# Linear attention and a snake MLP on one core: attention of each batch interleaved with the MLP products of earlier tokens

## The chip, the cores and the metric

The kernel runs on one core of one Trainium2 chip. The metric is the device time of one execution in microseconds, median over several runs. TensorE multiplies matrices; its results go to a memory of their own, PSUM, and a copy out of PSUM is called an eviction below. VectorE and ScalarE do arithmetic by rows and read PSUM and SBUF, the memory of the operands; GpSimd is given operands in SBUF alone in these kernels; DMA queues move data from and to the chip's main memory. The engines run side by side, each in its own order of instructions, and wait for one another by semaphores.

## The reference, cut to what matters

```python
# attention: batch 8, heads 8, sequence 576, head_dim 64
q_s = exp(q) / sum(exp(q), axis=-1)          # over head_dim (the maxima cancel)
k_s = exp(k) / sum(exp(k), axis=2)           # over the sequence
kv  = einsum('bhsd,bhse->bhde', k_s, v)
x   = einsum('bhsd,bhde->bhse', q_s, kv)     # then 4608 tokens x 512
# MLP: d_model 512, d_ff 2048
h = x @ w_in
g = h + sin(alpha * h)**2 / alpha            # "the gate" below
out = g @ w_out
```

## The kernel before: the parts that the change and the argument touch

Both kernels make bf16 operands, let exp go without its maximum, and keep x transposed (`xT`, model dimension on the partitions) for the MLP. Before, attention of all batches comes first, by chunks of 128 tokens and four heads; a scheduler orders the instructions.

```python
for b in range(B):
    for h0 in range(0, H, HG):                      # HG = 4 heads
        for ci, (s0, sc) in enumerate(s_sizes):     # 128, 128, 128, 128, 64 tokens
            # k on the sync queue, q (and v below) on the scalar queue: runs of 256 bytes
            nc.sync.dma_start(out=kqc[:sc, :HG], in_=k[b, h0:h0 + HG, s0:s0 + sc, :].rearrange("hh s d -> s hh d"))
            nc.scalar.activation(kqcb[:sc], kqc[:sc], AX.Exp)
            nc.vector.tensor_reduce(qs[:sc], qc[:sc], axis=AXL.X, op=ALU.add)
            nc.vector.reciprocal(qs[:sc], qs[:sc])
            nc.vector.tensor_tensor(qcb[:sc], qc[:sc], ...)                # divide q
            ...  # two transposes, each with its VectorE copy; sums of k by a product with ones
            ...  # VectorE cast of v; four kv products, 64 columns each
        ...      # VectorE: kv / sum of k, per head
        for si, sblk in enumerate(range(0, S, 512)):                       # per head
            nc.tensor.matmul(o_ps[pb:pb + D, :nfree], kv_sb[pb:pb + D, kp],
                             q_sbT[pb:pb + D, kp, sblk:sblk + nfree], start=True, stop=True)
            nc.vector.tensor_copy(xT_sb[pb:pb + D, ko, mbase:mbase + nfree], o_ps[pb:pb + D, :nfree])
...              # weights: one load and one ScalarE cast each
for mo in range(nMouter):                           # nine tiles of 512 tokens
    for ni in range(nN):                            # 16 blocks of 128 hidden units
        for ki in range(nK):                        # 4 products: h
            nc.tensor.matmul(h_ps, win_sb[:, ki, ...], xT_sb[:, ki, m0:m0 + MF], ...)
        nc.scalar.activation(s_sb, h_ps, AX.Sin, scale=a_col)
        nc.scalar.activation(s_sb, s_sb, AX.Square)
        nc.vector.scalar_tensor_tensor(g_all[:, ni], in0=s_sb, scalar=inva_col, in1=h_ps, ...)
    for j in range(MF // 128):                      # 4 x 16 output products
        ...
```

## Time and profile before

Time before: 480.73 us (median of 4 runs, 480.59 to 480.87).

| Stage of the kernel before | us | busiest engine |
|---|---|---|
| attention, eight batches | 0 to 217 | VectorE, 175.5 us busy |
| MLP, nine tiles | 217 to 479 | TensorE, 98% busy |

The view by windows gives the busy time of each engine in a stretch of the span, with the number of instructions, then the recorded clock of TensorE (1.00 is full speed), the DMA engines' share and GB/s. These are three stretches of the kernel before:

```profile
0.00:217.00 217.00, 100.73 (x768) 53.75 (x769) 175.50 (x706) 65.28 (x84) 0.70 (x6) 1.00 0.72 170
217.00:222.00 5.00, 4.97 (x13) 1.78 (x13) 0.00 (x0) 3.02 (x5) 0.00 (x0) 1.00 0.00 0
222.00:479.00 257.00, 252.12 (x1141) 108.94 (x1139) 126.88 (x180) 158.91 (x286) 0.00 (x0) 1.00 0.10 37
```

The order of the columns is TensorE products, weight loads, VectorE, ScalarE, GpSimd. The first stretch is attention: VectorE is the busiest at 175.5 of 217 us. The third is the MLP at TensorE's pace. The second is the first 5 us of the MLP.

The chain of waits of the kernel before, in order of time (start, length, what), two pieces of the MLP:

```profile
264.67 11.74 PE outp L169 x54
293.15 11.74 PE outp L169 x54
```

They repeat every 28.48 us: that is one tile, 128 products at 217 ns (11.74 us for 54) and little else.

### The profile page before, as it was taken

To read this page: it belongs to the slowest core of one execution; us is meant where nothing else is said; L and a number is where in the kernel's file an instruction comes from. 1 tells how busy PE (TensorE), PEld (TensorE's weight loads), DVE (VectorE), ACT (ScalarE), POOL (GpSimd) and SP (SyncE) were. 2 spreads that over 40 slices of the span, in tenths; PEclk is the share of its full clock that TensorE was granted. 3 is DMA by queue.
4 is the path that set the end of the run, shared out by engine and by line. 5 is a ranking of instruction groups with operands and counts; after the bars stand their busy time and mean duration, and the time that the engine had idled before them with its cause. 6 is when DMAs were issued, how large, how long until landed. Compare 5 with 4: busy or idle time off the path is not lost.

```text
span 479.4 us, 5928 instructions
## 1 busy us (share of the span) xinstructions
PE 357.8 (75%) x1920; PEld 164.5 (34%) x1920; DVE 302.4 (63%) x886; ACT 227.2 (47%) x373; POOL 0.7 (0%) x6
## 2 busy tenths in 40 slices
PE   1152355555555555559999999999999999999996
PEld 0120222222222222323444444444444444444442
DVE  2395589999999999994626355362644536455462
ACT  2130132322222227537829286491937739195680
POOL 0000000000000000000000000000000000000000
PEclk9999999999999999999999999999999999999999
DMA  9899697766677674500020100102011020101102
GB/s 266 259 205 339 169 174 178 171 155 152 149 157 175 149 164 93 123 2 0 0 89 0 67 22 26 64 0 87 2 45 46 3 86 0 67 22 46 44 1 88
DMA packets 124303, 46.54 MB, mean 97 GB/s; under 512 B 117104, under 2 KB 117104, under 8 KB 123760
## 3 DMA queue, kind: packets, MB, share of 16 engines
q1 hardware_dynamic: 47984, 27.28, 19.3%
q10 hardware_dynamic: 76288, 18.88, 18.2%
q8 instruction: 15, 0.25, 0.2%
q14 instruction: 16, 0.13, 0.1%
HBM read 36.71 MB, written 9.44 MB: 96 GB/s over the span
## 4 chain that ended last, share of the span: by engine, by line
PE 36%; DVE 25%; ACT 22%; DMA 9%; issue 7%; ACTq 0%; SPq 0%
PE outp L169 22%; ACT s_sb L162 13%; DVE xT_sb L124 10%; ACT s_sb L163 8%; DMA kqc<-in_q_dram 8%; DVE q_sbT L92 5%; PE h_ps L157 4%; PE o_ps L119 4%; PE qcT_ps L90 3%; DVE qcb L85 3%; PE kvps L102 3%; DVE v_sb L98 2%; DVE kv_sb L113 1%; DVE g_all L164 1%; DVE qs L82 1%
## 5 line engine op out<-in xcount | busy, mean ns | idle before, releaser
L164 DVE SCALAR_TENSOR_TENSOR g_all<-s_sb,inva_sb,h_ps 128x512 bf16<-128x512 f32 x144 | 102.0, 745 | 71.0 <-ACT s_sb L163 71.0
L157 PE MATMUL h_ps<-xT_sb,win_sb 128*128 128x512 bf16 x576 | 136.7, 383 | 2.5 <-DVE xT_sb L124 0.9
L169 PE MATMUL outp<-wout_sb,g_all 128*128 128x512 bf16 x576 | 135.3, 379 | 0.1
L162 ACT ACTIVATE s_sb<-h_ps,alpha_sb 128x512 f32<-128x512 f32 x144 | 94.0, 714 | 84.7 <-PE h_ps L157 84.7
L78 ACT ACTIVATE kqcb<-kqc 128x512 bf16<-128x512 f32 (+1 forms) x80 | 50.0, 629 | 137.5 <-DMA vf<-in_v_dram 39.7
L163 ACT ACTIVATE s_sb<-s_sb 128x512 f32<-128x512 f32 x144 | 85.7, 659 | 0.5
L157 PEld LDWEIGHTS <-win_sb 128*128 128x128 bf16 x576 | 56.6, 98 | 77.7 <-issue 17.5
L169 PEld LDWEIGHTS <-g_all 128*128 128x128 bf16 x576 | 54.2, 98 | 71.1 <-DVE g_all L164 9.4
L173 DVE COPY o_sb<-outp 128x512 f32<-128x512 f32 x36 | 24.9, 691 | 61.6 <-PE outp L169 61.6
L119 PE MATMUL o_ps<-q_sbT,kv_sb 64*64 64x64 bf16 (+1 forms) x128 | 37.1, 437 | 30.0 <-DVE kv_sb L113 24.7
L124 DVE CAST xT_sb<-o_ps 64x512 bf16<-64x512 f32 (+1 forms) x128 | 52.7, 451 | 8.2 <-PE o_ps L119 6.0
L102 PE MATMUL kvps<-v_sb,kqcb 128*64 128x64 bf16 (+1 forms) x320 | 25.9, 242 | 32.6 <-DVE v_sb L98 32.6
L90 PE MATMUL qcT_ps<-identb,qcb 128*128 128x128 bf16 (+1 forms) x160 | 29.7, 288 | 22.9 <-DVE qcb L85 21.6
L82 DVE TENSOR_REDUCE qs<-kqcb 128x4 f32<-128x256 bf16 (+1 forms) x80 | 32.3, 405 | 8.9 <-ACT kqcb L78 8.9
L102 PEld LDWEIGHTS <-kqcb 128*64 128x64 bf16 (+1 forms) x320 | 21.7, 135 | 44.4 <-issue 44.1
L93 PE MATMUL ksps<-ones,kqcb 128*128 128x1 bf16 (+1 forms) x160 | 14.2, 173 | 29.9 <-ACT kqcb L78 29.8
L92 DVE COPY q_sbT<-qcT_ps 128x128 bf16<-128x128 bf16 (+1 forms) x160 | 27.1, 210 | 14.5 <-PE qcT_ps L90 11.0
L85 DVE TENSOR_TENSOR qcb<-kqcb,qs 128x256 bf16<-128x256 bf16 (+1 forms) x80 | 33.3, 417 | 0.5
L119 PEld LDWEIGHTS <-kv_sb 64*64 64x64 bf16 x128 | 12.3, 134 | 41.1 <-DVE kv_sb L113 29.1
L98 DVE CAST v_sb<-vf 128x256 bf16<-128x256 f32 (+1 forms) x80 | 20.9, 265 | 6.8 <-DMA vf<-in_v_dram 6.7
L93 PEld LDWEIGHTS <-kqcb 128*128 128x128 bf16 (+1 forms) x160 | 9.5, 110 | 43.5 <-ACT kqcb L78 34.6
L90 PEld LDWEIGHTS <-qcb 128*128 128x128 bf16 (+1 forms) x160 | 10.4, 109 | 33.0 <-DVE qcb L85 32.0
(16 smaller groups left out, 52.8 us busy)
## 6 DMA issues: line engine op xcount, KB each, us to landing
out_dram<-o_sb SPq DMA_DIRECT2D x36, 256.0 KB, 2.0
kqc<-in_k_dram SPq DMA_DIRECT2D x64, 128.0 KB, 2.9
kqc<-in_q_dram ACTq DMA_DIRECT2D x64, 128.0 KB, 3.1
vf<-in_v_dram ACTq DMA_DIRECT2D x64, 128.0 KB, 2.8
tmp<-in_moe_w_in_dram SPq DMA_DIRECT2D x1, 4096.0 KB, 13.6
tmp<-in_moe_w_out_dram SPq DMA_DIRECT2D x1, 4096.0 KB, 18.4
kqc<-in_k_dram SPq DMA_DIRECT2D x16, 64.0 KB, 3.0
kqc<-in_q_dram ACTq DMA_DIRECT2D x16, 64.0 KB, 3.2
```

Source lines behind the costliest of these rows:

```text
L78: nc.scalar.activation(kqcb[:sc], kqc[:sc], AX.Exp)
L85: nc.vector.tensor_tensor(qcb[:sc], qc[:sc], qs[:sc].unsqueeze(2).to_broadcast([sc, HG, D]), op=ALU.mult)
L90: nc.tensor.transpose(qcT_ps[:, :sc], qcb[:sc, kp * 2:(kp + 1) * 2], identb[:sc, :sc])
L92: nc.vector.tensor_copy(q_sbT[:, kp, s0:s0 + sc], qcT_ps[:, :sc])
L102: nc.tensor.matmul(kv_ps_l[kp][pb:pb + D, hi % 2], kcb[:sc, hi], v_sb[:sc, hi], start=(ci == 0), stop=(ci == NC - 1))
L119: nc.tensor.matmul(o_ps[pb:pb + D, :nfree], kv_sb[pb:pb + D, kp], q_sbT[pb:pb + D, kp, sblk:sblk + nfree], start=True, stop=True)
L124: nc.vector.tensor_copy(xT_sb[pb:pb + D, ko, mbase:mbase + nfree], o_ps[pb:pb + D, :nfree])
L157: nc.tensor.matmul(h_ps, win_sb[:, ki, ni * 128:(ni + 1) * 128], xT_sb[:, ki, m0:m0 + MF], start=(ki == 0), stop=(ki == nK - 1))
L162: nc.scalar.activation(s_sb, h_ps, AX.Sin, scale=a_col)
L163: nc.scalar.activation(s_sb, s_sb, AX.Square)
L164: nc.vector.scalar_tensor_tensor(g_all[:, ni], in0=s_sb, scalar=inva_col, in1=h_ps, op0=ALU.mult, op1=ALU.add)
L169: nc.tensor.matmul(outp, g_all[:, ni, j * 128:(j + 1) * 128], wout_sb[:, ni, :], start=(ni == 0), stop=(ni == nN - 1))
```

## The change

The intent is to fill TensorE, which was half idle in attention, by running attention of batch t+1 among the MLP products of tile t, and to make attention cheaper: one load for a whole batch of q, k or v, nine neighbouring tokens on one partition (runs of 2304 bytes), few wide operations, kv products of even and odd heads on the upper and lower 64 rows of the array. The order of instructions is now written by hand: what the source issues first comes first on each engine. The heart of the change (the helpers are ordinary):

```diff
-            for ci, (s0, sc) in enumerate(s_sizes):
-                ...                                       # the loops shown above
+    ctx.enter_context(tc.manual_schedule())
+    stage = ... bufs=6      # loads;  ps_h 4 banks, ps_o 2 banks, ps_a ONE buffer of 2 banks
+    def src_view(t, b):
+        return t[b].rearrange("(i e) (p j) d -> (e p) i (j d)", e=2, j=J)     # J = 9
+    def kv_mm(b, ii, first):
+        for j in range(J):
+            for e in range(2):
+                r = slice(64 * e, 64 * e + 64)
+                nc.tensor.matmul(kvp[:, e, ii * 130:(ii + 1) * 130], ke[r, j, ...], vt[r, j, ...], ...)
+    # ... load_win(0..3) half on the sync, half on the scalar queue, beside q, k, v of batch 0
+    # ... batch 0's attention, then tile 0:
+    SQ0 = "APADAPADPADAPADP"               # who squares: ScalarE, GpSimd, VectorE
+    for ni in range(nN):
+        if ni % 4 == 0:
+            nc.vector.tensor_copy(win[:, :, c * 512:(c + 1) * 512], wst["i", c])   # weight cast
+            ...                                            # c = ni // 4; the next loads
+        hp = mm_h(0, ni)
+        snake(0, ni, hp, SQ0[ni])
+    for c in range(4):
+        nc.gpsimd.tensor_copy(wout[:, 4 * c:4 * c + 4, :], wst["o", c])
+    # ... 64 output products of tile 0; exp_q(1), exp_k(1); four evictions; norm_q(1), ...
+    for t in range(1, nT):
+        b = t + 1 if t + 1 < B else None
+        os = o_stream(t - 1) if t > 1 else None           # output products of the tile before
+        for ni in range(nN):
+            hp = mm_h(t, ni)                               # 4 products
+            snake(t, ni, hp, "A" if t > 1 else SQ0[ni])    # sine, square, gate
+            if b is not None:
+                if ni == 1:    exp_q(b); exp_k(b); cast_v(b, nc.gpsimd); load_batch(b + 1)
+                elif ni == 4:  norm_q(b, nc.gpsimd)        # VectorE row sums, GpSimd division
+                elif ni == 5:  kv_mm(b, 0, True); kv_mm(b, 1, False)
+                elif ni == 6:  kv_norm(b)
+                elif 8 <= ni < 11: q_transpose(b, ni - 8)  # 6 transposes, 1 VectorE copy
+                elif ni >= 12: attn_out(b, ni - 12, nc.vector.tensor_copy)
+            if os is not None:
+                ...                                        # 20 products at ni = 1, then 3 or 4 a block
+    for _ in o_stream(nT - 1): pass
```

## The prediction

> **What bounds it now.** The table by windows shows two stages. Attention runs from 0 to 217 us: VectorE is busy 65 to 81 us of each 87 us, TensorE about half: a VectorE chain of small pieces behind its DMA (packets almost all under 512 B). The MLP runs from 217 to 479 us with TensorE 99% busy, 28.49 us for each of nine 512-token tiles (pieces of the chain of waits), 217 ns per 128x512 product. Granted clock 0.998.
>
> **What the change does.** TensorE's floor becomes 1152 products x 217 ns = 250 us plus about 6 us per batch for kv, transposes and attention output (estimate from 4 kv products in 0.32 us and two transposes in 0.39 us): 298 us. VectorE's attention work goes into wide operations: per batch a 2304-element row reduction about 2.45 us (406 ns at 256 elements, slope 1 ns), evictions of transposed q about 2.2 us, of xT 3.6 us, normalisation 1 us. With 16 gate operations of 708 ns and four output copies of 691 ns it has 23 us in a tile: no longer the limit. The division of q goes to GpSimd. The small packets become 2304 B runs.
>
> **Why the floor is not reached.** Each engine's order is now fixed, so I laid out one tile (2 to 6) by hand with trace durations.
> - ScalarE: sine and square now alternate on one tile and cannot overlap: 0.71+0.66 = 1.4 us per block, against 1.25 now. At block 1 come four 1152-element exponentials (1.1 us each, from 629 ns at 512) between two table loads of 1.28 us: 7 us without a sine. Per tile about 30 us.
> - TensorE bridges this with 20 output products and four h buffers.
> - The row sums of q follow gate 4 on VectorE, at about +16 us after the second h block; then GpSimd divides 128x2304. No such operation is in this trace; the Trainium skill ("GPSIMD Engine Reference", section Elementwise) has about 2.6 cycles per element for two inputs, an estimate of 5 us. TensorE reaches the transposes at about +16.7 and waits until about +21: 4.5 us.
> - Transposes and attention outputs share one PSUM buffer, whose copy stands behind the gate of the same block, 2.2 us after its h. TensorE waits nearly 1 us at most of these: about 4 us together.
>
> Period about 42.5 us, five times: 213 us.
> Other stages: prologue with batch 0 alone 32 us; tile 0, limited by VectorE (gates, squares, weight casts), and its output product behind GpSimd's weight casts, until 70 us; batch 1's attention with nothing to overlap, because its row sums stand behind tile 0's evictions, until 91 us; tile 1 about 41 us (GpSimd squares stand behind the division). Tiles 7 and 8 at 28 us, last output product and store 17 us. Sum: 91+41+213+73 = 418; I take 415.
>
> **Predicted: 415 us, range 390 to 440 (8 in 10). Faster by over 2%: 0.96; within 2%: 0.03; slower: 0.01.**
>
> **In the profile:** TensorE idle before the transposes, ended by GpSimd's q product, 3 to 6 us per tile; idle before attention output ended by xT copies, about 1 us each; tile period 40 to 45 us for tiles 2 to 6 and 28 us for the last two; TensorE nearly idle from 70 to 90 us.
>
> **What would make it wrong:** a GpSimd product of 8 us or 3 us instead of 5 (4 us per tile either way); a table load that drains more than its 1.28 us; row-tiled kv products overlapping in pairs (1 us per tile less); slower first loads, since weight halves are issued beside q.

## More of the kernel before

Product by product, the first twelve of the MLP start 427 ns apart and the later ones 216 ns. The trace's record of the clock has its first entry at 221.9 us; before it there is none, and the view prints 1.00.

Two groups of TensorE products of the kernel before, kept apart by shape (columns: count, then busy us and mean ns of one, then idle time before them), both with 512 columns:

```profile
L119 PE MATMUL o_ps<-q_sbT,kv_sb 64*64 64x512 bf16 x64 | 34.6, 619 | 30.0 <-DVE kv_sb L113 24.7 <-DVE xT_sb L124 5.2
L157 PE MATMUL h_ps<-xT_sb,win_sb 128*128 128x512 bf16 x576 | 136.7, 383 | 2.5 <-DVE xT_sb L124 0.9
```

A product's duration, whose end the profile models, is longer than the spacing of products in a row. The same 512 columns take 619 ns in attention and 383 ns in the MLP. The smaller shape isn't the reason: the MLP's own first products take 634 ns each, and 379 once they come every 216 ns, and none of the 64 in attention took less than 579.

## The result, and the profile after

The changed kernel takes 440.23 us (median of 4 runs, 439.25 to 441.32). The ratio to the kernel before is 0.9157 (95% interval 0.9142 to 0.9172). Ratios are as recorded, from the fast runs of the same rounds, so not quite the ratio of the medians quoted.

So the change is faster by 8.4%, where 13.7% was predicted, and 440.23 lies just above the top of the stated range. The profile's page after, busy times and slices (each digit is the busy share of a fortieth of the span, in tenths; PEclk the recorded clock):

```profile
PE 317.4 (72%) x1621; PEld 147.8 (34%) x1649; DVE 210.1 (48%) x331; ACT 232.6 (53%) x326; POOL 58.1 (13%) x40
PE   0055566915754689588877969795889588999995
DVE  0545543073255634554646284628453665554531
PEclk9999668965765889899969997997899899999999
```

No engine is near full. The clock of TensorE is below full in much of the middle. By windows, after, for the stages in turn (tile 0's hidden blocks; its output products; batch 1; tile 1; then tile 2, cut from a little after its start to the same place in tile 3):

```profile
33.50:72.30 38.80, 23.85 (x64) 8.52 (x66) 19.07 (x25) 18.79 (x28) 5.96 (x6) 0.78 0.38 130
72.30:89.10 16.80, 15.61 (x63) 6.56 (x63) 0.65 (x3) 3.76 (x4) 8.81 (x6) 0.90 0.58 211
89.10:111.50 22.40, 6.98 (x62) 4.82 (x64) 11.88 (x18) 0.70 (x2) 0.00 (x0) 0.55 0.78 259
111.50:155.70 44.20, 26.19 (x127) 11.60 (x129) 21.85 (x36) 23.83 (x32) 12.22 (x9) 0.73 0.22 80
155.70:197.40 41.70, 33.63 (x182) 15.63 (x185) 20.69 (x35) 26.78 (x37) 7.65 (x5) 0.92 0.08 19
```

The chain of waits after shows the period of the full tiles by the table load ahead of each tile's exponentials:

```profile
161.25 1.28 ACT L121
203.15 1.28 ACT L121
244.88 1.28 ACT L121
286.48 1.28 ACT L121
328.09 1.28 ACT L121
```

41.6 to 41.9 us a tile, against 28.5 us in the MLP of before plus 27 us of attention for a batch (217/8). I had predicted 42.5. Stage by stage, with boundaries where the first work of a stage starts in the timelines (33.5, 89.1, 111.4, 154.3 and 364.6 us, good to half a microsecond):

| Stage | predicted us | measured us | difference |
|---|---|---|---|
| prologue, batch 0 | 32 | 33.5 | +1.5 |
| tile 0: h and output products | 38 | 55.6 | +17.6 |
| batch 1 | 21 | 22.3 | +1.3 |
| tile 1 | 41 | 42.9 | +1.9 |
| tiles 2 to 6 | 213 | 210.3 | -2.7 |
| tiles 7, 8, last output | 73 | 74.4 | +1.4 |
| sum | 418 | 439.0 | +21.0 |

Nearly all of the error is in one stage, tile 0. TensorE's timeline after, in tile 0 (start, length, what, how many; in brackets the idle time before, and what ended it):

```profile
35.22 5.80 PE L202 MATMUL hp<-xT,win 128*128 128x512 bf16 x15 [1.02 <-DVE win L266]
44.87 6.30 PE L202 MATMUL hp<-xT,win 128*128 128x512 bf16 x16 [3.85 <-DVE win L266]
54.91 6.39 PE L202 MATMUL hp<-xT,win 128*128 128x512 bf16 x16 [3.75 <-DVE win L266]
64.67 1.03 PE L202 MATMUL hp<-xT,win 128*128 128x512 bf16 x2 [3.36 <-DVE win L266]
```

Four blocks (16 products) at a time take 6.3 us, 0.39 us a product and not 0.22, and then TensorE stands idle for 3.4 to 3.9 us, until VectorE has cast the next quarter of the input weights. That cast stands in VectorE's order behind the gates of the four blocks before it, so TensorE is done with its four blocks before the cast can begin. Product by product, those of the first three bursts start 427 ns apart until 4.8 to 5.6 us into the burst, and 216 ns apart for the last two or three. The same view in the middle of tile 2:

```profile
174.51 1.03 PE L202 MATMUL hp<-xT,win 128*128 128x512 bf16 x4
179.94 0.79 PE L180 MATMUL tp<-identb,qn 128*128 128x128 bf16 x6 [4.40 <-POOL qn L144]
181.80 1.84 PE L202 MATMUL hp<-xT,win 128*128 128x512 bf16 x4
184.45 1.03 PE L202 MATMUL hp<-xT,win 128*128 128x512 bf16 x4
193.00 0.41 PE L188 MATMUL xp<-qT,kvb 128*128 128x256 bf16 x2 [1.20 <-DVE xT L192]
```

Here is the predicted wait for GpSimd's q product, 4.40 us (4.5 predicted), and one of the waits for a copy. What I had not put in: after those 4.40 us the next four h products take 1.84 us, before and later 1.03.

### The profile page after: what moved, and what is told of

The parts are those of the page before. It is cut to its first block, busy times and chain, and to the rows that moved or that the text cites. A ratio compares the mean times of both kernels' runs of the same rounds, so it can differ in the third digit from the quotient of the medians.

```text
span 439.0 us, 4398 instructions
## 1 busy us (share of the span) xinstructions
PE 317.4 (72%) x1621; PEld 147.8 (34%) x1649; DVE 210.1 (48%) x331; ACT 232.6 (53%) x326; POOL 58.1 (13%) x40
## 4 chain that ended last, share of the span: by engine, by line
PE 42%; ACT 21%; DVE 15%; issue 10%; POOL 6%; DMA 2%; POOLq 1%; SPq 0%; ACTq 0%; DVEq 0%
PE hp L202 19%; PE op L219 16%; ACT s L208 9%; POOL qn L144 5%; ACT s L210 4%; DVE g L215 3%; DVE xT L192 3%; PE tp L180 3%; ACT ke L121 3%; DVE qs L141 2%; ACT L121 2%; DMA st_k<-in_k_dram 2%; ACT qe L121 2%; ACT L208 2%; PE hp L219 2%
## 5 line engine op out<-in xcount | busy, mean ns | idle before, releaser
L215 DVE SCALAR_TENSOR_TENSOR g<-s,inva_sb,hp 128x512 bf16<-128x512 f32 x144 | 106.3, 745 | 158.9 <-ACT s L210 139.4
L202 PE MATMUL hp<-xT,win 128*128 128x512 bf16 x569 | 165.7, 422 | 20.0 <-DVE win L266 12.0
L208 ACT ACTIVATE s<-hp,alpha_sb 128x512 f32<-128x512 f32 x144 | 98.2, 684 | 121.4 <-PE hp L202 106.8
L219 PE MATMUL op<-wout,g 128*128 128x512 bf16 x523 | 140.6, 392 | 4.7 <-POOL wout L277 3.8
L202 PEld LDWEIGHTS <-win 128*128 128x128 bf16 x576 | 61.4, 108 | 96.4 <-issue 30.2
L219 PEld LDWEIGHTS <-g 128*128 128x128 bf16 x576 | 57.0, 101 | 73.3 <-issue 15.4
L210 ACT ACTIVATE s<-s 128x512 f32<-128x512 f32 x126 | 79.4, 630 | 4.0
L144 POOL TENSOR_TENSOR qn<-qe,qs 128x2304 bf16<-128x2304 bf16 x6 | 24.3, 4047 | 171.4 <-ACT s L210 160.6
L224 DVE COPY o<-op 128x512 f32<-128x512 f32 x34 | 22.9, 676 | 29.4 <-PE op L219 29.4
L188 PE MATMUL xp<-qT,kvb 128*128 128x256 bf16 x64 | 15.2, 324 | 23.7 <-DVE xT L192 19.1
L192 DVE CAST xT<-xp 128x256 bf16<-128x256 f32 (+1 forms) x56 | 22.8, 448 | 5.8 <-PE xp L188 5.8
L121 ACT ACTIVATE ke<-st_k 128x1152 bf16<-128x1152 f32 x16 | 17.6, 1146 | 0.0
```

The source lines that it names most:

```text
L121: nc.scalar.activation(dst[:, :, ii * 128:(ii + 1) * 128].rearrange("p j (x d) -> p x j d", x=2), src[:, ii::2], AX.Exp)
L144: eng.tensor_tensor(qn.rearrange("p j (i d) -> p (j i) d", i=4), qe3, qs.unsqueeze(2).to_broadcast([128, J * 4, D]), op=ALU.mult)
L188: nc.tensor.matmul(op[:, half, 0:(j1 - j0) * P], kt[:, hp, :], qT[:, j0:j1, ii, e * 64:(e + 1) * 64], start=True, stop=True)
L192: eng(xT[:, hp, c0:c0 + (j1 - j0) * P], op[:, half, 0:(j1 - j0) * P])
L202: nc.tensor.matmul(hp, win[:, ki, ni * 128:(ni + 1) * 128], xT[:, ki, t * MF:(t + 1) * MF], start=(ki == 0), stop=(ki == 3))
L208: nc.scalar.activation(s, hp, AX.Sin, scale=alpha_sb[:, ni:ni + 1])
```

## The experiments

My theory after the result: (a) tile 0 loses to the place of the weight casts in VectorE's order, (b) idle spells of TensorE cost twice, since its products run at half speed for a while after them, (c) the full tile loses to three orderings that can be repaired one by one. The rivals stand with each run. Every kernel gave a correct result.

### Weight casts out of VectorE's order, and the clock by itself

```diff
 # e1_cast_pool
+    for c in range(4):
+        nc.gpsimd.tensor_copy(win[:, :, c * 512:(c + 1) * 512], wst["i", c])
     for ni in range(nN):
-        if ni % 4 == 0: nc.vector.tensor_copy(win[:, :, c * 512:(c + 1) * 512], wst["i", c])
```

> Edit: the four casts of the input weights go to GpSimd, all ahead of tile 0, instead of standing in VectorE's order after every fourth gate. In the changed kernel tile 0's 16 blocks took 38.8 us (33.5 to 72.3 us) where I had predicted about 20, with TensorE's granted clock at 0.75. Theory A (each cast stands behind the gates of the four blocks before it, so TensorE runs dry for 3.8 us four times, and the dry spells hold its clock at half): tile 0 falls to 22 to 27 us, no idle of TensorE before h ended by the weight cast, total 424 to 430. Rival B (the half clock comes from the idle prologue and stays whatever the casts do): the 64 products still take 427 ns, tile 0 about 30 us, total 431 to 434.

```diff
 # e2_spin: order kept; products of zeros into an unread PSUM tile
+    def spin(n):
+        d = ps_o.tile([128, dm], F32, name="spin", tag="o")
+        for i in range(n): nc.tensor.matmul(d, identb, kvz, start=(i == 0), stop=(i == n - 1))
         snake(0, ni, hp, SQ0[ni])
+        if ni % 4 == 3: spin(12)          # and 60, 30 and 24 at the three other places
```

> Edit: nothing is moved; TensorE gets useless products of zeros in its idle spells (60 before batch 0's transposes, 12 after every fourth block of tile 0, 30 before batch 1's transposes, 24 in tile 1 before the transposes), to see what the half clock alone costs. If the clock is a secondary cost (theory A): clock over tile 0 from 0.75 to 0.95 or more, tile 0 from 38.8 to 30 to 33 us since the casts still drain it, tile 1 from 45.6 to 40 to 42, total 427 to 432. If the clock is nearly all of it (rival B): tile 0 about 22 us, total below 422. If the spells are set by the casts alone and the clock costs nothing: total within 3 us of 440.

Measured: 422.33 us without the casts in VectorE's order, a little better than the 424 to 430 expected, and 429.74 us with the spin, as expected. The timelines of TensorE in tile 0, first with the casts on GpSimd, then with the spin:

```profile
35.76 7.63 PE L202 MATMUL hp<-xT,win 128*128 128x512 bf16 x27 [0.22 <-issue]
43.55 3.77 PE L202 MATMUL hp<-xT,win 128*128 128x512 bf16 x16 [0.16 <-DVE g L215]
47.47 2.78 PE L202 MATMUL hp<-xT,win 128*128 128x512 bf16 x11 [0.16 <-DVE g L215]
```

```profile
44.14 3.63 PE L209 MATMUL hp<-xT,win 128*128 128x512 bf16 x16 [1.55 <-DVE win L275]
47.60 2.75 PE L83 MATMUL spin<-kvz,identb 128*128 128x512 bf16 x11
52.27 3.63 PE L209 MATMUL hp<-xT,win 128*128 128x512 bf16 x16 [1.92 <-DVE win L275]
```

From the first h product to the first output product of tile 0: 38.2 us in the changed kernel (35.2 to 73.4), 32.2 with the spin (35.3 to 67.5), 20.6 with the casts moved (35.8 to 56.4). With the spin, 16 products take 3.63 us instead of 6.3, and the useless 12 cost nothing, since TensorE would stand there anyway; but it still waits for the cast. So both parts of theory (a, b) hold here: the spin takes away 6.0 us of half speed, and moving the casts takes away 17.6 us in all. Without them TensorE is hardly idle, and slow only for the first 2.8 us (the full clock is recorded from 38.6 us). That run changes the casts' engine as well as their place; the four casts are 4.9 us of VectorE's work, and VectorE was idle for half of this stage, so its load alone can't be the 17.6 us. The rival that the clock is nearly everything expected less than 422 us with the spin, and falls. Tile 1 also gained from the spin: the table loads of tiles 1 and 2 lie 41.9 us apart, against 45.4.

### Copies ahead of the gate

```diff
 # e4_copy_first, tiles 1 to 6
             hp = mm_h(t, ni)
+            if 8 <= ni < 11: q_transpose(b, ni - 8)
+            elif ni >= 12: attn_out(b, ni - 12, nc.vector.tensor_copy)
             snake(t, ni, hp, ...)
```

> Edit: in tiles 1 to 6 the transposes and attention outputs, with their copies out of PSUM, are issued before the gate of the same block instead of after it; TensorE's order stays, VectorE's copy no longer waits for the block's sine, square and gate. My prediction had these waits as about 4 us of each 41.7 us period. Theory: period 37 to 38.5 us in tiles 2 to 6, idle before attention output ended by xT copies nearly gone (19 us in total before), total 418 to 424. Rival (the wait for GpSimd's q product and ScalarE's lag set the period, and the copy waits are slack behind them): period 41 us or more, total above 436.

Measured: 419.91 us; table loads of tiles 3 and 4 in its chain of waits, the longest of its full tiles:

```profile
195.68 1.28 ACT L121
234.69 1.28 ACT L121
```

Over tiles 1 to 6 (118.1 to 310.7 us) the period is 38.5 us on average, where it was 42.5 (115.8 to 328.1 us in the changed kernel); over tiles 2 to 6 alone it is 38.2, where it was 41.7. TensorE's waits for xT copies before attention outputs fell from 19.1 us in all (16 times) to 5.3 (6 times). TensorE's order did not change; VectorE only no longer takes a block's gate, which waits for sine and square, ahead of a copy that could go at once and that holds TensorE's only PSUM buffer for attention. The rival, slack behind the other waits, falls.

### Division of q two blocks earlier

```diff
 # e5_early_norm
-                elif ni == 4:
+                elif ni == 2:
                     norm_q(b, nc.gpsimd)
```

> Edit: the row sums and the division of q are issued after block 2 of a tile instead of after block 4; all else as in the changed kernel. There TensorE waits 4.4 us in each of five tiles before the first transposes, for GpSimd's q product. Theory (that product starts when the row sums come up in VectorE's order, so starting them two blocks of 1.4 us earlier shortens the wait by about 2.8 us): wait 1.5 to 1.8 us, period from 41.7 to 38.5 to 39.5 us, total 422 to 429. Rival (the wait only moves to the copies of the transposed q or to ScalarE): period 41 us or more, total above 436.

Measured: 416.19 us, a larger saving than expected. The lines of the table of waits for TensorE's weight loads before the transposes (total us, times, longest), first the changed kernel, then this one:

```profile
PEld L180 <- POOL qn L144: 24.4, 5, 4.9
```

```profile
PEld L180 <- POOL qn L144: 9.0, 5, 1.8
```

The wait fell from 4.9 us at most to 1.8, as expected, and the period to 37.5 us (193.13, 230.67, 268.22 in the chain). That is 4.1 us less, where the wait gave 3.1: the h products after the shorter wait take 1.03 us for four, not 1.84. Mean recorded clock 0.931 instead of 0.891. The transposes now wait for kv's normalisation on VectorE, 1.33 us in tile 2; so a part did move, as the rival said, but a small one.

### Batch 1 among tile 0's output products

```diff
 # e6_overlap_b1
+    exp_q(1); exp_k(1); norm_q(1, nc.vector); cast_v(1, nc.gpsimd)
     for ni in range(nN):
         for j in range(4): mm_o(0, j, ni, accs[j])
+        if 9 <= ni < 12: q_transpose(1, ni - 9)
+        elif ni == 12: kv_mm(1, 0, True); kv_mm(1, 1, False); kv_norm(1)
+        elif ni >= 14: attn_out(1, ni - 14, nc.vector.tensor_copy)
     for j in range(4): evac_o(0, j, accs[j], nc.vector.tensor_copy)
-    norm_q(1, nc.vector); ...              # all of batch 1 came here
+    for hp in range(2, 4): attn_out(1, hp, nc.scalar.copy)
```

> Edit: batch 1's row sums, division and casts are issued before tile 0's output products instead of behind their four evictions, and its transposes, kv products and two attention outputs are spread among those products. In the changed kernel 22.9 us lie between the last output product of tile 0 (89.0 us) and the first h of tile 1 (111.9 us), with TensorE busy 6.4 of 20 us. Theory: these fall to 5 to 8 us, total 423 to 427. Rival (the stage is set by the loads of batch 1 or by the weight casts on GpSimd): less than 5 us gained, total above 435.

Measured: 423.84 us, 16.4 us less, as expected. Between the last output product of tile 0 and the first h of tile 1 lie 2.8 us (93.9 to 96.7), fewer than the 5 to 8 expected. The row sums had stood behind the four evictions in VectorE's order, and the evictions behind the last output product; nothing in the data asked for that.

### Interleaving undone, the new attention kept

```diff
 # e8_serial
+    for b in range(B):
+        exp_q(b + 1); exp_k(b + 1); cast_v(b + 1, nc.gpsimd); load_batch(b + 2)
+        q_transpose(b, 0..2); norm_q(b + 1, nc.gpsimd); kv_mm(b, 0..1); kv_norm(b); attn_out(b, 0..3)
+    ...                                     # weights loaded, cast on GpSimd
     for t in range(nT):
-        b = t + 1 if t + 1 < B else None
+        b = None                            # no attention among the blocks
```

> Edit: the interleaving is undone and all else of the change kept: attention of all eight batches first (whole-batch loads, wide operations, row-tiled kv products, GpSimd for the division and the casts of v), then weights, then the MLP with the output products of the tile before. Theory (interleaving is where the gain comes from): 440 us or more. Rival (the gain comes from the rewritten attention, and interleaving in this order gives some of it back): about 14 us a batch, attention done near 135 us, MLP about 261 us, total 390 to 405.

Measured: 388.97 us, 51 us below the changed kernel that it takes the interleaving out of. By windows, a batch of attention and a tile of the MLP:

```profile
65.00:80.00 15.00, 7.11 (x62) 4.80 (x62) 7.80 (x16) 5.62 (x8) 6.80 (x4) 1.00 0.70 252
213.00:241.00 28.00, 27.89 (x130) 12.70 (x130) 14.36 (x20) 21.45 (x33) 0.00 (x0) 1.00 0.18 41
```

The row sums repeat every 14.46 us here (32.94, 47.39, 61.86 us in the chain of waits), attention ends near 129 us where it took 217 before, and the MLP takes its 258 us. So the gain of the change comes from the rewritten attention: 88 of the 92 us from 480.7 to 389.0 are saved before the MLP. The changed kernel gives 51 us of it back, but not all of them through interleaving: this run also casts the input weights on GpSimd, which alone gave 17.9 us (e1), and issues their loads late, so that its first exponential starts at 5.1 us instead of 12.5. My estimate from these is about 26 us for interleaving in the written order; no run tests that alone. This is the finding that the prediction did not contain: I had compared with the old attention only.

### The repairs together

`e7_all` joins e1, e4, e5 and e6, puts the transposes at blocks 9 to 11, and lets VectorE take over GpSimd's squares in tile 1.

> Edit: input-weight casts on GpSimd ahead of tile 0, copies ahead of the gate, division of q after block 2 with transposes at blocks 9 to 11, batch 1 among tile 0's output products, and no GpSimd squares in tile 1. If the losses are separate, as my account has them, they add up: 18 us (weight casts, measured), 20 us (copies, measured), about 14 us each for the other two, and some for a TensorE clock that no longer drops: period 33 to 35 us, granted clock above 0.96, total 360 to 378. If they hide one another (fixing one exposes the next wait): 385 us or more, no better than the kernel without interleaving at 389.

Measured: 351.95 us (351.23 to 352.36), below the expected 360 to 378. The single savings against 440.23 are 17.9, 20.3, 24.0 and 16.4 us, 78.6 together; this kernel saves 88.3. They add up and a little more, so they did not hide one another. The other 9.7 us may come from the two further edits, the later transposes and tile 1's squares, which no run tests alone. A tile of it, by windows:

```profile
153.64:186.00 32.36, 31.22 (x192) 15.25 (x191) 22.12 (x37) 27.52 (x39) 6.26 (x3) 1.00 0.43 139
```

TensorE is busy 31.2 of 32.4 us, at the full clock. The interleaving now pays: 37 us less than the serial form, although its weight loads still stand early.

### Row tiling, and the size of the packets

```diff
 # e10_rows_apart
-        for j in range(J):
-            for e in range(2):
+        for e in range(2):
+            for j in range(J):
```

> Edit: the kv products, which alternate between the upper and the lower 64 rows of the array in the changed kernel, are issued as nine on one half and then nine on the other. A look at whether row-tiled products overlap: at the full clock 18 of them took 0.68 us, 38 ns each, below the 55 ns that 130 columns take at the measured 217 ns for 512. Theory (halves run at the same time): about 1.0 us for 18 products. Rival (a product with 64 rows is simply shorter): 0.7 us. Either way under 1 us a batch, total within 4 us of 440.

The timelines of the 36 kv products of one batch, first the changed kernel, then this one:

```profile
211.38 1.20 PE L154 MATMUL kvp<-vb,ke 64*128 64x130 bf16 x36
```

```profile
215.36 1.59 PE L154 MATMUL kvp<-vb,ke 64*128 64x130 bf16 x36
```

The Trainium skill ("TensorE: Matmul & The Clock Gate", Part 3) says that products on different row groups run at the same time. The trace agrees, and the start times of the single products show it. In the changed kernel two products, one on each half, start 3 or 4 ns apart, and the pairs follow one another every 57 ns or so. With the halves apart, products of one half start about 56 ns apart, so a pair takes no longer than one product, and the rival (a product with 64 rows is simply shorter) falls. It's less than I expected (1.59 us, not 2.0, for 36) because the runs of nine overlap: each starts 303 ns after the one before it, when three of that one's nine are still to start. Alternating halves saves 0.39 us a batch. The timeline is of the slower execution, but these products have the spacing of the full clock. The two timed runs gave 444.71 (slow, by its distance from the other) and 432.80 us; both lie outside the expected 4 us around 440, and why is open. The total says nothing about an effect of 0.39 us a batch.

```diff
 # e11_small_packets: tokens p, p+64, ... on partition p; runs of 256 B, eight loads of 64 partitions
-        return t[b].rearrange("(i e) (p j) d -> (e p) i (j d)", e=2, j=J)
+        return [t[b].rearrange("(i e) (j p) d -> e p i j d", e=2, j=J)[e] for e in range(2)]
```

> Edit: only the order of tokens within a batch changes: partition p holds tokens p, p+64, ... instead of nine neighbours, so the loads of q, k and v fall back from runs of 2304 B to runs of 256 B (as in the kernel before), by eight loads of 64 partitions each instead of one; operations and their order stay. Before reached 174 to 266 GB/s with such runs, so a batch of 3.5 MB takes 14 to 20 us of a 41.7 us period. Theory (long runs do not carry the gain once loads are hidden under a tile): prologue 2 to 6 us longer, the rest unchanged, total 441 to 447. Rival (they matter throughout): above 455.

Measured: 454.10 us, 13.9 us more, between the two expectations. The packets, ScalarE's issues of three weight loads, and the table load ahead of the first exponential, in the changed kernel and in this one:

```profile
DMA packets 22821, 46.43 MB, mean 106 GB/s; under 512 B 1792, under 2 KB 1808, under 8 KB 22800
0.73 10.40 ACTq L108 DMA_DIRECT2D st_w<-in_moe_w_in_dram  x3
11.16 1.28 ACT L121 ACT_TABLE_LOAD   x1 [11.16 <-DMA st_k<-in_k_dram]
```

```profile
DMA packets 123768, 46.47 MB, mean 103 GB/s; under 512 B 115024, under 2 KB 115040, under 8 KB 123744
11.66 11.01 ACTq L105 DMA_DIRECT2D st_w<-in_moe_w_in_dram  x3
22.77 1.28 ACT L118 ACT_TABLE_LOAD   x1 [22.77 <-DMA st_v<-in_v_dram]
```

11.6 us are lost before the first exponential, another 3.7 by the exponentials of tile 1, and nothing later in the full tiles, whose period is 40.8 to 41.1 us. So long runs do not carry the gain in the full tiles, as the theory had it, and the loss before the first exponential is twice to six times what I wrote for the prologue.

That loss isn't the landing of q: q's last piece landed at 10.1 us here and at 9.0 in the changed kernel, but the exponentials began at 24.1 and 12.5. Ahead of them in ScalarE's order stand three issues of weight loads, and these wait for a semaphore each. The third went out at 10.53 us in the changed kernel, when the first half of k had landed at 10.51, and at 22.07 here, when the fourth piece of v had landed at 22.05. That these landings released them is read from the times. Eight issues for one load, which keep the queue busy for 5.5 us a tensor, put more landings ahead of the weights. What runs of 256 B cost by themselves this run doesn't show.

### A version that beats both

`e12_final` adds two things to `e7_all`: input weights are loaded after batch 0's exponentials instead of beside its q and k, and three output products go ahead of a tile's first h.

> Edit: the kernel with all five repairs (352 us), and in addition the loads of the input weights are issued after the exponentials of batch 0 instead of beside its q and k, and at a tile's start three output products go ahead of the first h, which waits 0.9 us for the last xT copy. Expected: first exponential from 12.6 us to 8 to 9.5 us, the 0.9 us wait gone in five tiles, total 343 to 349. If the loads of weights then come late for tile 0's first products, the first of these is lost again and the total is 348 to 352.

Measured: 342.23 us (341.54 to 343.41), ratio to the kernel before 0.7099 (0.7080 to 0.7119), slightly better than expected. The first exponential starts at 5.7 us instead of 12.6, right after the first half of q has landed (5.72 us): the issues of weight loads no longer stand ahead of it. Tile 2's table load lies at 111.3 us instead of 118.2, so this edit gives most of the gain over `e7_all`. The period is 32.0 us (143.75, 175.78, 207.82) instead of 32.3: the wait of the first h at a tile's start is gone, but one in mid-tile grew from 0.6 to 1.0 us. Against the serial form, whose weight loads are late too, this kernel takes 47 us less. It is 29% below the kernel before and 22% below the changed one.

## Why the prediction was wrong, point by point

- **Direction, mechanism of the full tile: right.** Period 42.5 predicted, 41.7 measured; wait for the q product 4.5 predicted, 4.4 measured; waits for copies "about 1 us each" measured at 0.8 to 1.2. Tiles 7 and 8 at TensorE's pace: right. Batch 1 alone with TensorE idle: right, 22.3 us for 21, though 20 us later than I wrote. Of the 21 us between my sum and the trace, these stages hold about 3.
- **The step that failed: "tile 0, limited by VectorE (gates, squares, weight casts), and its output product behind GpSimd's weight casts, until 70 us".** I summed VectorE's work and took the sum, about 20 us, for tile 0's 16 blocks. The sum was right: VectorE is busy 19.07 of the 38.8 us that they took. But an engine's busy time bounds a stage only if the engine is never kept waiting. Here a cast waits for gates, gates for ScalarE, ScalarE for TensorE, TensorE for that cast: a ring with one quarter of the weights in it at a time. I had laid out one full tile instruction by instruction, and had not done so for tile 0. Moving the casts out of the ring, and to GpSimd, took 17.6 us off this stage and 17.9 off the total, and accounts for nearly all that was missing.
- **"Granted clock 0.998": the record was believed, the durations not read.** In the profile of before, 512 columns took 619 ns in attention and 383 in the MLP, and the MLP's first twelve products came every 427 ns, the later ones every 216. TensorE ran at half speed for 220 us where the view said 1.00. The Trainium skill ("TensorE: Matmul & The Clock Gate", "What's actually happening") says the half rate is the default, that about 3.4 us of sustained work bring the full rate, and that an idle window takes it back. This agrees: after idle spells of 3.8 us, 16 products take 6.3 to 6.4 us; with gaps of 1.3 to 1.9 us they take 3.63. The moment varies: in the four bursts of tile 0 the full rate is recorded 4.8, 5.4, 5.6 and 2.7 us after the first product. In the prediction this cost is absent; the spin run puts it at 6.0 us in tile 0, and 3.5 us in tile 1.
- **Errors that cancelled in the full tile.** I took attention as 6 us of TensorE a batch from products that ran at half speed. At full speed kv is 1.20 us, the transposes about 1.0 (0.34 from a group of six to the product after it) and the outputs about 1.0 (0.25 from a pair to the product after it). The half clock after each wait, which I had left out, cost 0.8 us and more. GpSimd's division took 4.05 us instead of the estimated 5. And that sine and square "cannot overlap", 1.4 us per block, was wrong: in the first tile of the serial form a block takes 1.24 us, less than the 0.69 and 0.63 of the two.
- **The range was too narrow, for a nameable reason:** 25 us either way was set by doubts about one tile's period, and that was the part I had worked out. The doubt belonged to the stages I had estimated from sums.

What stays open: what short runs cost without the issues that come with them, how the 51 us of the serial form split between interleaving and weights, and what the two further edits of `e7_all` are worth.

## What to carry to other kernels

When a stage is ordered by hand, its time is not the busiest engine's sum but the longest ring of waits: check for each operation what stands ahead of it in its engine's order that it doesn't need, and put short copies that free a buffer ahead of long chains. Compare an interleaved kernel with a serial one of the same parts: interleaving paid only after its order was repaired, and here it had cost about 26 us by estimate, in a kernel 51 us slower than its serial form. Look in the same way at what stands ahead of the first operation, DMA issues on a computing engine included. And read TensorE's speed from the duration of equal products, in every stage, before trusting a clock column.

## What the Trainium skill lacked or had wrong

- "TensorE: Matmul & The Clock Gate", "Seeing it yourself", warns that clock events can be unreliable. It lacks a form seen here: before the first recorded change the profile's views read 1.00 while products run at half speed. In the kernel before, 512 columns took 619 ns over 217 us at a recorded 1.00; in the serial form, 36 kv products took 2.13 us at a recorded 1.00 and 1.20 us elsewhere. The mean clock inherits this: four runs of the serial form, 388.9 to 389.5 us, have means of 0.955, 0.996, 0.999 and 0.899.
- The same page says that the full rate needs sustained work. It warns of idle gaps above about 3 us (gaps of 1.3 to 1.9 us between bursts did keep the full rate in the spin run), but gives no share of busy time that brings the rate. Attention with TensorE busy about half the time reached it once in 129 us, for 3.4 us, where two output products took 283 and 299 ns, and the next two 369 and 471 (the serial form).
- "GPSIMD Engine Reference", section 3.1, gives about 2.6 cycles an element for two inputs, measured with fp32, and no figure for bf16. The division here, bf16 with one operand broadcast, took 4.05 us for 2304 elements, 2.1 cycles at the page's 1.2 GHz; the squares of 512 fp32 elements took 1.04 us, 2.4 cycles.
- "ScalarE: Activation LUTs", "What ACT_TABLE_LOAD costs", gives 2.66 us for a switch, of which 1.38 us is a drain. Here the exponential began 0.02 us after a table load of 1.28 us (load at 115.81, exponential at 117.11), and the load 0.01 us after the sine before it: 1.3 us in all.
